# Twelve of an expert's fourteen weight loads move from the join to the next expert's first tile

## The chip, the cores and the metric

The kernel runs on one core of a Trainium2 chip. The metric is device microseconds of one execution, and the number that counts is the median of several runs. TensorE (PE) multiplies, VectorE (DVE) and ScalarE (ACT) do the element work, GpSimd (POOL) issues the indirect transfers, SyncE (SP) issues the plain ones.

## The reference

Causal attention (4 batches, 12 heads, 448 positions, 64 wide) gives 1792 rows of 768. Two mixture-of-experts layers follow, each with 8 experts whose weights are 768x1024 and 1024x768. In the first layer a row is computed only if its skip score is above 0; each row goes to the one expert with the largest logit:

```
for e in range(E):
    mask = e_idx == e
    h = np.maximum(xc[mask] @ w1[e], 0.0)
    y[mask] = gate_w[mask, None] * (h @ w2[e])
out[do_compute] = xc + y
```

The second layer does the same with all rows, normalised logits and other weights, and without adding the row itself.

## The kernel before

The attention is written out first and takes about the first 230 us. The rest is 16 experts, 8 of each layer, in one order written out by hand for every engine (`tc.manual_schedule`). An expert's rows are taken in tiles of 128 by an indirect gather. How many tiles an expert has is known only at run time: `Tile.begin` and `Tile.finish` of a first tile are always there, further tiles stand in a branch (`tc.If(nmore[e] > 0)`, line 1107, and the tests of `middle`, line 1088). Behind the branch the paths join again, and there stands one `tile.finish(at_end, True, ...)` for whichever tile was the last of the expert (line 1118).

A tile works in this order on TensorE. `begin`: `layer1` (line 781) makes two halves of 512 columns from six chunks of w1, first the terms with the high part of the weights, then those with the low part; the halves are copied (line 940), turned (line 798) and split by ReLU into high and low (lines 772, 773); then `layer2` (line 789) goes through chunks 0 to 5 of w2. `finish`: the next tile's rows are turned and split (lines 754, 760, 761) between `layer2` of chunks 6 and 7, and the result is scaled and written out by `put_y`. In the first layer the routing of the second (`route_...`) is woven into the same tiles: `route_turn` (line 834, copied by ACT at line 835), `route_logits` (line 840), and a write of the row to `x2` (line 856).

Weights come in as float32 (`raw`) and are split into a rounded high part by ACT (line 736) and the remainder by DVE (line 740). The remainder overwrites the raw chunk. There are 14 rooms for w1 chunks (`N1`, six chunks per expert) and 16 for w2 chunks (`N2`, eight per expert), so a load at expert i brings chunks 2 to 5 of w1 of expert i+2, chunks 0 and 1 of w1 of expert i+3, and all of w2 of expert i+2. A w1 chunk is 512 KB, a w2 chunk 384 KB. `load1` (line 212) and `load2` (line 218) issue on SP's queue, which in this stage carries nothing but these loads and SP's own branches. Each waits until the products that read the old content of its room are done.

In an expert's first tile the high parts of w2 are made at `w2_high(0, 1, 2, 3)` (in `begin`, before the first products), `w2_high(4)` and `w2_high(5, 6, 7)`; those of the next expert's w1 at `ahead(0)`, `ahead(1)` and, in `finish` of the last tile, `high(2)` to `high(5)`.

`paced(load, after)` can put a load behind a named instruction; in the kernel before no call passes one.

Between the layers stands a turn (lines 1137 to 1158): the last rows are routed, `dispatch` gathers the first tile of expert 8 (line 743, by `first`), and TensorE runs products of zeros (`busy`, line 129) in the meantime.

Of the kernel before, what the change touches and what calls it, by code (L numbers as in the profile page):

```python
# [26 lines left out]
KC = DM // P  # L27
FC = DF // P
# [17 lines left out]
def moe_attention_kernel(tc, qk, vv, w_r, emb, tau, w11, w12, w21, w22, out):  # L46
    nc = tc.nc
# [24 lines left out]
    with ExitStack() as top:  # L72
# [135 lines left out]
        def load1(n, after=None):  # L208

            if n < len(experts) * KC:  # L210
                (m, e), k = experts[n // KC], n % KC
                paced(nc.sync.dma_start(raw1[n % N1], wsrc[m][0][e, k * P : (k + 1) * P, :]), after)

        def load2(n, after=None):

            if n < len(experts) * FC:
                (m, e), f = experts[n // FC], n % FC
                paced(nc.sync.dma_start(raw2[n % N2], wsrc[m][1][e, f * P : (f + 1) * P, :]), after)
# [466 lines left out]
        with ExitStack() as ctx:  # L685
# [7 lines left out]
            for n in range(FC, N2):  # L693
# [20 lines left out]
            gate2 = keep([P, 1], F32, "gate2")  # L714
            norms = (keep([P, 1], F32, "ss2"), keep([P, 8], F32, "ex2"), keep([P, 1], F32, "gs2"),
                     keep([P, 1], I32, "tn_y"), keep([P, 1], F32, "tn_a"))
            state = {"tp": 0}

            def next_tp():
                state["tp"] = (state["tp"] + 1) % 3  # L720
# [54 lines left out]
            def layer1(i, u, ks, low):  # L775

                for k in ks:
                    wh, wl, _ = w1(i, k)
                    terms = [(0, wl)] if low else [(0, wh), (1, wh)]
                    for j, r in terms:  # L780
                        nc.tensor.matmul(p1[u], xt[:, k, :, j], r[:, u * 512 : (u + 1) * 512],  # L781
                                         start=(k == 0 and j == 0 and not low), stop=(k == KC - 1 and low))

            def layer2(i, f, us=(0, 1)):
                wh, wl, _ = w2(i, f)
# [156 lines left out]
            class Tile:  # L942
# [23 lines left out]
                def ahead(self, k):  # L966

                    if self.first and self.i + 1 < len(experts):
                        split_high(self.i + 1, k)
                        split_low(self.i + 1, k, nc.vector)  # L970

                def begin(self):
                    i, route = self.i, self.m == 0 and self.prev
                    if self.m == 1 and self.prev:
                        put_out()
                    self.step()
                    self.w2_high(0, 1, 2, 3)
                    layer1(i, 0, range(4), False)
                    layer1(i, 1, range(3), False)
                    layer1(i, 0, range(4, KC), False)  # L980
                    self.step()
                    layer1(i, 0, range(KC), True)
                    if route:

                        route_enter()
                    self.w2_low(0, 1)
                    copy_h(0)
                    self.w2_high(4)
                    self.step()
                    self.w2_low(2, 3)  # L990
                    self.step()
                    layer1(i, 1, range(3, KC), False)
                    if i == 0 and not self.prev:
                        late_hots()
                        enter_late()
                    if route:
                        route_turn()
                    state["tp"] = 2
                    turned = turn_h(0)
                    self.step()  # L1000
                    split_ht(turned, 0)
                    while self.norm:
                        self.step()
                    layer1(i, 1, range(KC), True)
                    copy_h(1)
                    self.w2_high(5, 6, 7)
                    if route:
                        route_logits()
                    self.w2_low(4)
                    if route:  # L1010
                        route_pick()
                    self.w2_low(5)
                    layer2(i, 0)
                    layer2(i, 1)
                    turned = turn_h(1)
                    split_ht(turned, 4)
                    self.w2_low(6, 7)
                    layer2(i, 2)
                    layer2(i, 3)
                    if route:  # L1020
                        route_rank()
                    self.ahead(0)
                    self.ahead(1)
                    layer2(i, 4)
                    layer2(i, 5)

                def finish(self, idx, last, nxt, route):
                    i = self.i
                    more = last and i + 1 < len(experts)
                    state["tp"] = 1  # L1030

                    def high(*ks):
                        for k in ks:
                            if more:
                                split_high(i + 1, k)

                    def low(*ks):
                        for k in ks:
                            if more:
                                split_low(i + 1, k, nc.vector)  # L1040

                    if last:
                        for k in range(KC):
                            load1(KC * i + k + N1)
                        for f in range(FC - 2):
                            load2(FC * i + f + N2)
                    if nxt is not None:
                        t = xt_turn(nxt, *HALVES[0])
                        xt_split(t, *HALVES[0])
                    high(2)  # L1050
                    layer2(i, 6)
                    if nxt is not None:
                        t = xt_turn(nxt, *HALVES[1])
                        xt_split(t, *HALVES[1])
                    low(2)
                    high(3)
                    low(3)
                    layer2(i, 7)
                    if last:
                        load2(FC * i + 6 + N2)  # L1060
                        load2(FC * i + 7 + N2)
                    high(4, 5)
                    low(4, 5)
                    if route:
                        route_put()
                    put_y(self.m, self.g, idx)

            def run_layer(m, info, ir):
                L, _, _, nmore, several = info
                for e in range(NE):  # L1070
                    i, c0 = m * NE + e, e * CT

                    prev = e > 0

                    def rows(t):
                        return L[:, c0 + t : c0 + t + 1]

                    gr, gr2 = g_r[e % 2], g_r[(e + 1) % 2] if e + 1 < NE else None
                    at_end = ir[:, e : e + 1]
                    tc.mark_branch_hint_location(f"more{i}", several[e], engines=list(nc.engines))  # L1080
                    if gr2 is not None:
                        gather(m, gr2, rows(CT))
                    gather(m, g_n[1], rows(1))
                    tile = Tile(i, gr, True, prev)
                    tile.begin()

                    def middle(t):
                        with tc.If(nmore[e] > t):  # L1088
                            g = g_n[t % 2]
                            if t <= NMID:  # L1090
                                g2 = g_n[(t + 1) % 2]
                                gather(m, g2, rows(t + 1))
                                mid = Tile(i, g, False, True)
                                mid.begin()
                                mid.finish(rows(t), False, g2, m == 0)
                                middle(t + 1)
                            else:
                                with tc.For_i(t, nmore[e], 1) as u:
                                    nc.vector.tensor_copy(ix, L[:, bass.ds(u + c0, 1)])
                                    gather(m, g, ix)  # L1100
                                    make_xt(g)
                                    mid = Tile(i, g, False, True)
                                    mid.begin()
                                    mid.finish(ix, False, None, m == 0)
                                make_xt(gr)

                    with tc.If(nmore[e] > 0, label=f"more{i}"):
                        if m == 1:
                            gather(m, gr, at_end)
                        tile.finish(rows(0), False, g_n[1], m == 0 and prev)  # L1110
                        if m == 0:
                            gather(m, gr, at_end)
                        middle(1)
                        end = Tile(i, gr, False, True)
                        end.begin()
                        if m == 0 and not prev:
                            route_put()
                    tile.finish(at_end, True, gr2, m == 0 and prev)

            with tc.manual_schedule():  # L1120
# [86 lines left out]
```

## Time and profile before

| what | us |
|---|---|
| median of 3 runs (901.76 to 904.38) | 903.12 |
| the profiled execution's own time | 902.78 |
| its span, first to last instruction | 901.1 |
| TensorE busy in it | 824.0 |
| VectorE busy | 554.4 |
| ScalarE busy | 474.8 |

The profiled execution is 0.34 us under the median and lies 1.7 us over its own span. The mean granted TensorE clock is 0.978 of full speed. TensorE is busy in nearly all of the span, so idle stretches of the other engines cost something only where TensorE ends up waiting for them.

### The profile page before, as it was taken

What the parts mean: (1) busy time and instruction counts of PE and PEld (TensorE: products, weight loads), DVE (VectorE), ACT (ScalarE), POOL (GpSimd) and SP (SyncE); (2) the same over time, 40 slices, a digit from 0 to 9 for tenths busy, and PEclk for the clock granted to TensorE, in tenths of its full rate; (3) what the DMA queues carried; (4) which work ended last, traced back from release to release, by engine and by line L of the source; (5) the groups of instructions that cost most, each with busy time, mean ns of one, the idle gap of its engine ahead of it and who ended that gap; (6) DMA issues with size and microseconds to landing.
All of it is one profiled execution on the core that took longest, in us unless ns stands there. A gap on an engine that the chain in (4) does not pass through costs nothing. (4 is left out here: it accounts for less than half of the span.)

```text
span 901.1 us, 14898 instructions
## 1 busy us (share of the span) xinstructions
PE 824.0 (91%) x4960; PEld 686.5 (76%) x4960; DVE 554.4 (62%) x1641; ACT 474.8 (53%) x1013; POOL 135.2 (15%) x150
## 2 busy tenths in 40 slices
PE   7998989989797899899999879899999998999994
PEld 5665766666487788788899748789889887889884
DVE  5767767776566688378833476665283268574343
ACT  5777666666455466166612336454272256463252
POOL 1132404013201111011010021011111011110100
PEclk9999999999899899999999999999999999999998
DMA  8979565563636487267710354580451086361000
GB/s 243 315 271 299 165 185 165 167 206 139 202 140 258 175 300 286 72 232 300 299 45 28 145 198 159 197 332 21 149 211 51 19 313 267 133 238 41 37 1 18
DMA packets 59032, 158.22 MB, mean 176 GB/s; under 512 B 13013, under 2 KB 23765, under 8 KB 58448
## 3 DMA queue, kind: packets, MB, share of 16 engines
q1 hardware_dynamic: 52816, 139.33, 43.4%
q0 software_dynamic: 6080, 17.29, 5.4%
q8 instruction: 59, 0.97, 0.5%
q14 instruction: 77, 0.63, 0.2%
HBM read 146.45 MB, written 22.92 MB: 188 GB/s over the span
## 5 line engine op out<-in xcount | busy, mean ns | idle before, releaser
L789 PE MATMUL p<-hi,ht 128*128 128x384 f32 x960 | 241.8, 353 | 8.5 <-DVE ht L773 4.6
L740 DVE TENSOR_TENSOR lo<-raw,hi 128x768 fp32r<-128x768 f32 (+1 forms) x218 | 220.6, 1062 | 8.0 <-ACT hi L736 4.5
L781 PE MATMUL p<-hi,xt 128*128 128x512 f32 x720 | 183.3, 403 | 8.0 <-PEq L1088 3.3
L736 ACT CAST hi<-raw 128x768 fp32r<-128x768 f32 (+1 forms) x218 | 187.3, 923 | 0.6 <-DMA raw<-in_w 0.6
L789 PEld LDWEIGHTS p<-hi,ht 128*128 128x128 f32 x960 | 167.8, 191 | 14.7 <-DVE ht L773 10.6
L781 PEld LDWEIGHTS p<-hi,xt 128*128 128x128 f32 x720 | 140.4, 198 | 37.4 <-ACTq L1088 5.1
L321 ACT ACTIVATE pr<-st,mn 112x336 f32<-112x336 f32 x192 | 99.5, 520 | 60.4 <-DVE mn L318 60.4
L789 PE MATMUL p<-lo,ht 128*128 128x384 f32 x480 | 124.3, 340 | 0.4 <-issue 0.4
L773 DVE SCALAR_TENSOR_TENSOR ht<-tp,ht 128x512 fp32r<-128x512 f32 x60 | 41.4, 689 | 115.3 <-ACT ht L772 106.6
L781 PE MATMUL p<-lo,xt 128*128 128x512 f32 x360 | 96.2, 402 | 0.0
L940 ACT COPY hs<-p 128x512 f32<-128x512 f32 x60 | 34.8, 580 | 106.0 <-PE p L781 67.0
L789 PEld LDWEIGHTS p<-lo,ht 128*128 128x128 f32 x480 | 88.7, 191 | 0.5 <-issue 0.5
L760 ACT CAST xt<-tp 128x384 fp32r<-128x384 f32 (+2 forms) x62 | 30.4, 492 | 109.5 <-PE tp L754 108.8
L761 DVE TENSOR_TENSOR xt<-tp,xt 128x384 fp32r<-128x384 f32 (+2 forms) x62 | 33.3, 544 | 84.5 <-ACT xt L760 81.6
L318 DVE CUSTOM_DVE_ANT_0 st<-s,mask 112x336 f32<-112x336 f32 x144 | 63.5, 465 | 29.4 <-PE s L307 17.8
L781 PEld LDWEIGHTS p<-lo,xt 128*128 128x128 f32 x360 | 67.8, 195 | 11.4
L772 ACT ACTIVATE ht<-tp 128x512 fp32r<-128x512 f32 x60 | 36.0, 600 | 55.1 <-PE tp L798 49.4
L331 PE MATMUL tp<-ident,pr 112*112 112x112 f32 x480 | 57.3, 267 | 0.0
L307 PE MATMUL s<-qk 64*112 64x112 f32 (+2 forms) x288 | 49.6, 450 | 7.1 <-DVE mn L318 7.1
L331 PEld LDWEIGHTS tp<-ident,pr 112*112 112x112 f32 x480 | 47.1, 136 | 8.6 <-issue 7.8
L818 POOL DMA_INDIRECT out<-py,pidx x18 | 19.7, 1093 | 207.7 <-ACT hi L736 75.5
L342 PE MATMUL av<-pt,v 112*64 112x448 f32 (+3 forms) x384 | 50.6, 405 | 0.0
(201 smaller groups left out, 908.3 us busy)
## 6 DMA issues: line engine op xcount, KB each, us to landing
raw<-in_w SPq DMA_DIRECT2D x96, 512.0 KB
raw<-in_w SPq DMA_DIRECT2D x128, 384.0 KB
qk<-in_qk SPq DMA_DIRECT2D x23, 896.0 KB
x<-x SPq DMA_DIRECT2D x24, 448.0 KB
v<-in_vv SPq DMA_DIRECT2D x4, 1344.0 KB
qk<-in_qk SPq DMA_DIRECT2D x2, 448.0 KB
g_n<-x,L POOLq DMA_INDIRECT x23, 4.4
out<-py,pidx POOLq DMA_INDIRECT x18, 3.4
```

The lines of the kernel that those rows point to most:

```text
L307: nc.tensor.matmul(a[c], src[r : r + 64, c * CP : (c + 1) * CP], src[r : r + 64, S : S + n], start=True, stop=True)
L318: nc.vector.tensor_tensor_reduce(out=so, in0=a[c], in1=mask[:, S - n : S], scale=-0.125, scalar=3.0e38, op0=ALU.add, op1=ALU.min, accum_ou ...
L321: return lambda: nc.scalar.activation(a["pr"][:, OFF[c] * CP : OFF[c] * CP + n], so, AF.Exp, bias=mn, scale=-1.0, accum_out=rs)
L331: nc.tensor.transpose(tp[:, u * CP : (u + 1) * CP], pr[:, o : o + CP], ident[:CP, :CP])
L342: nc.tensor.matmul(av[u * D : (u + 1) * D, j * CP :], v_t[b][:, j, 2 * hp + u, :], pts[2 * g + u][:, o : o + (NCH - j) * CP], start=(j == ...
L736: copy(hi, raw)
L740: eng.tensor_tensor(lo, raw, hi.bitcast(F32), op=ALU.subtract)
L772: nc.scalar.activation(hi, src, AF.Relu)
L773: nc.vector.scalar_tensor_tensor(lo, src, 0.0, hi.bitcast(F32), op0=ALU.max, op1=ALU.subtract)
L781: nc.tensor.matmul(p1[u], xt[:, k, :, j], r[:, u * 512 : (u + 1) * 512], start=(k == 0 and j == 0 and not low), stop=(k == KC - 1 and low))
L789: mm = nc.tensor.matmul(p2[u], l, r[:, u * (DM // 2) : (u + 1) * (DM // 2)], start=(f == 0 and j == 0), stop=(f == FC - 1 and j == len(ter ...
L940: nc.scalar.copy(hs[:, u * 512 : (u + 1) * 512], p1[u])
```

## The change

Of the fourteen loads that `finish` issued at the join, the first two w1 chunks stay. The other four w1 chunks and the eight w2 chunks are put in a list. The first tile of the next expert takes one of them behind each of twelve pieces of its products: four pieces of `layer1` with high parts and low parts of the first half and the start of the second, two more of the second half, and `layer2` of chunks 0 to 5. Each load then waits, by `paced`, for the last product of its piece. `layer1` now returns the name of its last product.

```diff
-            state = {"tp": 0}
+            state = {"tp": 0, "loads": []}
+
+            def feed(after):
+
+                if state["loads"]:
+                    load, n = state["loads"].pop(0)
+                    load(n, after)
...
-                        nc.tensor.matmul(p1[u], xt[:, k, :, j], r[:, u * 512 : (u + 1) * 512],
+                        mm = nc.tensor.matmul(p1[u], xt[:, k, :, j], r[:, u * 512 : (u + 1) * 512],
                                          start=(k == 0 and j == 0 and not low), stop=(k == KC - 1 and low))
+                return mm.ins.name
...
+                def feed(self, after):
+                    if self.first:
+                        feed(after)
...
-                    layer1(i, 0, range(4), False)
-                    layer1(i, 1, range(3), False)
-                    layer1(i, 0, range(4, KC), False)
+                    self.feed(layer1(i, 0, range(4), False))
+                    self.feed(layer1(i, 1, range(3), False))
+                    self.feed(layer1(i, 0, range(4, KC), False))
...
-                    layer1(i, 0, range(KC), True)
+                    self.feed(layer1(i, 0, range(KC), True))
...
-                    layer1(i, 1, range(3, KC), False)
+                    self.feed(layer1(i, 1, range(3, KC), False))
...
-                    layer1(i, 1, range(KC), True)
+                    self.feed(layer1(i, 1, range(KC), True))
...
-                    layer2(i, 0)
-                    layer2(i, 1)
+                    self.feed(layer2(i, 0))
+                    self.feed(layer2(i, 1))
...
-                    layer2(i, 2)
-                    layer2(i, 3)
+                    self.feed(layer2(i, 2))
+                    self.feed(layer2(i, 3))
...
-                    layer2(i, 4)
-                    layer2(i, 5)
+                    self.feed(layer2(i, 4))
+                    self.feed(layer2(i, 5))
...
                     if last:
-                        for k in range(KC):
-                            load1(KC * i + k + N1)
-                        for f in range(FC - 2):
-                            load2(FC * i + f + N2)
+                        load1(KC * i + N1)
+                        load1(KC * i + 1 + N1)
+                        state["loads"] = [(load1, KC * i + k + N1) for k in range(2, KC)]
+                        state["loads"] += [(load2, FC * i + f + N2) for f in range(FC)]
...
-                    if last:
-                        load2(FC * i + 6 + N2)
-                        load2(FC * i + 7 + N2)
```

The first tile of an expert comes before its branch in every engine's order, so the twelve loads are issued whether the expert has one tile or more. The first tile of expert 0 finds the list empty.

## Rows read from the trace of the kernel before

**Rows 1.** The page: busy time of the engines.

```profile
PE 824.0 (91%) x4960; PEld 686.5 (76%) x4960; DVE 554.4 (62%) x1641; ACT 474.8 (53%) x1013; POOL 135.2 (15%) x150
```

**Rows 2.** Stretches, one tile each: length; busy by engine; clock; DMA share; GB/s.

```profile
core 0: us, PE busy (x) PEld busy (x) DVE busy (x) ACT busy (x) POOL busy (x), PEclk, DMA share, GB/s
263.83:291.43 27.60, 22.48 (x120) 19.91 (x120) 19.68 (x33) 16.37 (x24) 3.45 (x3) 0.95 0.74 277
291.43:319.63 28.20, 24.29 (x121) 21.96 (x121) 19.14 (x39) 14.76 (x22) 3.46 (x3) 0.87 0.49 191
388.83:411.18 22.35, 20.94 (x121) 18.71 (x120) 19.77 (x40) 15.60 (x23) 3.45 (x3) 1.00 0.48 183
411.18:433.53 22.35, 20.94 (x121) 18.73 (x121) 19.78 (x40) 15.62 (x23) 4.49 (x4) 1.00 0.79 304
```

**Rows 3.** Timeline of PE, experts 1, 2 and 6: start, length, what, idle before.

```profile
279.43 0.65 PE L798 MATMUL tp<-ident,hs 128*128 128x128 f32 x4 [2.38 <-ACT hs L940]
287.26 0.52 PE L754 MATMUL tp<-ident,g_r 128*128 128x128 f32 x3 [2.74 <-DVEq L1107]
305.16 1.20 PE L840 MATMUL pm<-wr,yt 128*128 128x8 f32 x6 [3.22 <-ACT yt L835]
...
408.40 0.52 PE L754 MATMUL tp<-ident,g_r 128*128 128x128 f32 x3 [1.24 <-DVEq L1107]
```

**Rows 4.** Timeline of ACT, experts 1, 2 and 6.

```profile
278.79 0.58 ACT L940 COPY hs<-p 128x512 f32<-128x512 f32 x1 [5.91 <-issue]
304.63 0.48 ACT L835 COPY yt<-tp 128x384 f32<-128x384 f32 x1 [4.86 <-issue]
...
421.35 0.58 ACT L940 COPY hs<-p 128x512 f32<-128x512 f32 x1 [0.82 <-PE p L781]
```

**Rows 5.** Timeline of SP at the join of expert 0.

```profile
260.69 2.78 SPq L212 DMA_DIRECT2D raw<-in_w  x6
263.58 8.94 SPq L218 DMA_DIRECT2D raw<-in_w  x8
```

**Rows 6.** Short stretches (columns as in rows 2; the last three: clock, DMA share, GB/s).

```profile
276.00:278.00 2.00, 1.05 (x6) 0.73 (x5) 0.37 (x2) 0.00 (x0) 0.66 (x1) 1.00 1.02 378
278.00:280.00 2.00, 0.57 (x5) 0.58 (x6) 0.00 (x0) 1.21 (x2) 0.00 (x0) 1.00 0.20 72
302.00:304.00 2.00, 0.00 (x0) 0.00 (x0) 0.00 (x0) 0.00 (x0) 0.00 (x0) 1.00 0.25 87
318.00:334.00 16.00, 15.82 (x91) 14.08 (x90) 14.90 (x34) 12.86 (x19) 3.46 (x3) 1.00 1.01 384
```

**Rows 7.** The page: a DMA queue that brings instructions (packets, MB, share).

```profile
q14 instruction: 77, 0.63, 0.2%
```

**Rows 8.** The turn: timelines of POOL, DVE and PE.

```profile
524.00 0.99 POOL L856 DMA_INDIRECT x<-py,pidx  x1 [12.23 <-DVE eq L848]
530.12 1.45 POOL L743 DMA_INDIRECT g_r<-x,first  x1 [5.13 <-DMA x<-py,pidx]
...
527.37 0.22 DVE L197 TENSOR_SCALAR first<-pm,tok 128x1 int32<-128x1 f32 x1 [0.30 <-PE pm L878]
...
534.61 1.54 PE L754 MATMUL tp<-ident,g_r 128*128 128x128 f32 x6 [2.77 <-DMA g_r<-x,first]
```

**Rows 9.** Line 856, all its writes to x2: landing times.

```profile
DMA to landing us min/median/max: 2.5/3.1/3.3
```

**Rows 10.** Stretches around the turn (columns as in rows 2).

```profile
517.00:526.00 9.00, 6.77 (x43) 4.92 (x42) 6.59 (x26) 4.87 (x9) 0.99 (x1) 1.00 1.02 407
530.00:537.60 7.60, 4.83 (x20) 3.44 (x18) 5.70 (x9) 2.00 (x5) 4.13 (x3) 0.78 0.37 107
```

**Rows 11.** Timelines of PE and ACT in expert 7's first tile.

```profile
433.53 4.35 PE L781 MATMUL p<-hi,xt 128*128 128x512 f32 x18
451.33 0.51 PE L789 MATMUL p<-hi,ht 128*128 128x384 f32 x2
...
444.18 2.30 ACT L736 CAST hi<-raw 128x768 fp32r<-128x768 f32 x3
```

**Rows 12.** Branches: PE timeline at expert 4's second tile; a stretch over a join.

```profile
365.58 1.86 PE L781 MATMUL p<-hi,xt 128*128 128x512 f32 x6 [0.96 <-DVEq L1088]
...
594.00:598.00 4.00, 4.00 (x23) 3.70 (x22) 2.63 (x4) 3.98 (x6) 0.00 (x0) 1.00 1.02 417
```

More of the change, by code (lines that the diff above doesn't have):

```diff
@@ L1117, in run_layer @@
                             route_put()
+                    assert not state["loads"]
                     tile.finish(at_end, True, gr2, m == 0 and prev)
```

## The prediction

> **What bounds the kernel now.** I read the page first: TensorE is busy 824.0 of 901.1 us [rows 1], so a change that adds and removes no product can only win or lose in TensorE's idle stretches and in its clock. The second view is a table of stretches, each from the first product of one tile to that of the next [rows 2]. The reader should compare the lengths. Single-tile experts of the first layer take 22.35 us with the DMA engines 48% busy and 22.35 us with them 79% busy: transfers as such slow nothing. But the tiles of experts 1 and 2 take 27.60 and 28.20 us for the same 120 or so products. They are 5.25 and 5.85 us too long, 11.10 us together.
>
> The third view, TensorE's timeline, shows where [rows 3]. In expert 1's tile it waits 2.38 us for ACT's copy of the second half (line 940) and 2.74 us at the join, where 1.24 us is usual. In expert 2's it waits 3.22 us for ACT's copy at line 835. The first two give 2.38 + (2.74 - 1.24) = 3.88 us; the rest is the clock, granted at 0.95 and 0.87 of full speed in these stretches and 1.00 in the others [rows 2]: 0.05 x 27.60 = 1.4 us, together 5.3 us, as found. For expert 2, 3.22 us and 0.13 x 28.20 = 3.7 us make 6.9 us, less what the shorter join gives back.
>
> Now ACT's own timeline [rows 4]. It is idle for 5.91 us before the one copy and 4.86 us before the other, and both times the releaser is "issue": it waited for no semaphore that the profile shows. In expert 6 the same copy starts after 0.82 us, as soon as TensorE is done. So something withholds ACT's next instruction. The short stretches say what ends it [rows 6]: up to 278 us the DMA engines are full (share 1.02), in the next 2 us they fall to 0.20, and ACT goes on at 278.79; in 302 to 304 us they are at 0.25, and ACT goes on at 304.63. Instructions come over DMA queues too [rows 7], and what fills the engines is the burst: SP issues fourteen loads within 11.8 us of the join [rows 5], 6 x 512 KB + 8 x 384 KB = 6.29 MB, which at 384 GB/s [rows 6] take 16.4 us. My reading: a block of ACT's instructions, asked for near the join, stands behind that burst, and ACT stops when it comes to the block's edge before the block is there. In the other experts the edge falls elsewhere or the block was fetched ahead of the burst.
>
> **The change part by part.**
>
> *The burst is cut to two loads.* 1.05 MB at 384 GB/s take 2.7 us, so a block asked for at the join is there some 3 to 4 us later, well ahead of the copies, which come 10 us and more behind the join. Later, four loads of 512 KB come behind pieces that end about 1.9 to 6 us after the first product (the first eighteen products of the first three pieces take 4.35 us [rows 11]): 2.10 MB, 5.5 us of transfer, so a queue of about 2 us at most. The last eight come about one per 1.2 us, each worth 1.02 us. Nothing stands long enough to hold back ACT by 5 us. I take both tiles down to the usual 22.35 us: -11.1 us. Bounds: 0 (the cause is another one) and -11.1.
>
> *The turn between the layers.* Expert 7's burst keeps the DMA engines at 1.02 in 517 to 526 us [rows 10]. The write to `x2` issued at 524.00 holds up the gather of expert 8's first rows until 530.12 [rows 8], 6.1 us, where such writes land after 2.5 to 3.3 us [rows 9]. TensorE then waits 2.77 us for that gather [rows 8], and the clock is at 0.78 over 7.6 us around it [rows 10], 1.7 us. With only two loads there, the write lands by 524.00 + 3.3 = 527.3 and the next thing late is `first`, ready at 527.37 + 0.22 = 527.59 [rows 8]. The gather could move up by 530.12 - 527.6 = 2.5 us; most of that and part of the clock come back. I take -3 us, with bounds 0 and -4.4 (2.77 and 1.7).
>
> *The loads come later: does a split wait?* The last load goes out when the twelfth piece ends, at 451.33 + 0.51 = 451.84 in expert 7's first tile. Its user is the last of the three casts that start at 444.18, at about 445.7 [rows 11], one whole tile later: 445.7 + 22.35 = 468.1 us for a single-tile expert, the tightest case. That leaves 16.2 us for a transfer of 1.02 us. The first w1 chunk of the list is due a whole tile after its piece. All fourteen need 16.4 of 22.35 us of DMA time. Cost 0; were the cover gone, a late chunk would show as ACT waiting for `raw`.
>
> *Twelve waits on SP.* What is queued behind a waiting load is the next load and SP's branches; no other engine waits for SP but through the loads' landing, just priced. Issue is about 0.46 us a load (2.78 us for six [rows 5]), off the path. POOL's gathers and writes keep their order, and share the DMA engines with loads in the second half of the tile that were there in the first half before. TensorE gets no instruction that I can see: its products already signal to others. 0.
>
> *The end of the first tile.* This is new: loads now run until shortly before each first tile's branch, where the engines jump and need the code behind the jump. At such a branch with empty DMA engines TensorE waits 0.96 us for another engine's jump, and at the join of expert 9, with the DMA engines full (1.02), it is busy all 4.00 of 4.00 us [rows 12]. So a full DMA need not hurt there. Low end 0; high end: the last two loads (0.79 MB, 2.0 us) stand in front of the code at each of the 14 first tiles that issue loads (experts 1 to 14) and nothing covers it, +28 us. The row with full engines is the nearest, and the products of two more w2 chunks still follow the last load; I take +1.5 us in all.
>
> *Sum.* 902.78 (the profiled execution, 0.34 us under the median) - 11.1 - 3 + 1.5 = 890.2; against the median 890.5 us.
>
> What speaks against this is a rule of the Trainium skill, page "Runtime: NRT & Kernel Launch", section "Instruction fetch mechanics": the sequencer fetches its next block over a DMA queue of its own while it runs the present one, and the cost of crossing a block's edge is "mostly hidden". By that rule the two ACT stops would not be code at all, and the sum would lose its first term. The trace speaks against it: it has two idle stretches of about 5 us with no semaphore behind them, which the rule does not explain. The same page's remark that a taken branch breaks the fetching ahead fits a block asked for only at the join; no row here shows when it was asked for.
>
> **The rivals.**
>
> *Only part comes back.* ACT's block is asked for later than I think, or meets the four 512 KB loads (5.5 us of transfer): one of the two stops stays, 5.3 to 5.9 us, or the turn gives nothing. For it: the rows show when ACT went on, not when it asked. 902.8 - 5.5 - 1.5 + 1.5 = 897 us. Chance 0.17.
>
> *The stops have another cause.* ACT would stop in experts 1 and 2 whatever DMA does, or the waits for TensorE come out so that the loads still leave together. Against it: twice the engines drained just before ACT went on. The turn's gain and the branch's cost stay: 902.8 - 3 + 1.5 = 901.3 us. Chance 0.11. This is where that page's rule leads, too.
>
> *Slower: the code at the branch.* Each first tile's last loads hold up the code behind its branch. It decides from about 1 us per first tile beyond what the last two w2 chunks' products cover: 14 x 1.0 us cancels the gain of 14.1, and at the full 2.0 us the time is 902.8 - 14.1 + 28 = 917 us. Against it: the full engines at expert 9's join. Chance 0.08.
>
> **How the numbers follow.** The forecast has 0.64: 890.5 us, and its own range is 886.5 to 896 (both gains whole, or the branch costs up to 5 us more). The range 886.5 to 899.5 takes in the partial case, 0.81 together. A measurement of this kernel can tell about 0.3%, 2.7 us: 900.4 to 905.8 is no change. Faster: forecast, partial case and a little of the third, 0.82. Same: 0.10. Slower: 0.08.
>
> **What would show it.** Right: the tiles of experts 1 and 2 at 22.3 to 23 us with the clock at 1.00; no ACT idle of over 2 us ended by "issue" there; SP's twelve loads spread over some 18 us of each first tile; the gather of expert 8's first rows at about 528 us on the old scale; TensorE's waits at lines 1088 and 1107 no longer than now. Wrong: the same two ACT stops beside half-empty DMA engines, ACT or DVE waiting for `raw`, or TensorE waits of 2 us at every first tile's end.

## The result, and the profile after

The changed kernel takes 907.72 us (median of 20 runs) against 903.15 us for the kernel before (20 runs): the ratio is 1.0051, 95% interval 1.0031 to 1.0071. It is slower by about half a per cent, where 890.5 us and a gain were forecast. The profiled execution took 907.67 us with a span of 906.0 us, 4.9 us over the span of before.

The page shows first that the work is the same and only its timing has moved:

```profile
PE 827.5 (91%) x4960; PEld 688.5 (76%) x4960; DVE 554.6 (61%) x1641; ACT 474.6 (52%) x1013; POOL 137.7 (15%) x150
...
q1 hardware_dynamic: 52816, 139.33, 46.4%
```

The second line is SP's loads: packets, MB and the share of the DMA engines' time. The bytes are those of before. TensorE is busy for 3.5 us more with the same 4960 products [rows 1], so most of the 4.9 us are products at the lower clock (mean 0.972, before 0.978) and about 1.4 us are idle time. The next view is the table of stretches, one tile each, with the columns of [rows 2]: experts 1 and 2, expert 6, then the first and second tiles of experts 4, 9 and 13.

```profile
262.75:288.77 26.02, 22.34 (x120) 20.13 (x120) 19.18 (x33) 15.91 (x23) 6.63 (x3) 0.93 0.77 257
288.77:316.95 28.18, 23.97 (x121) 21.69 (x121) 19.62 (x39) 15.23 (x23) 3.46 (x3) 0.88 0.63 203
...
408.81:431.75 22.94, 20.95 (x120) 18.74 (x120) 19.77 (x40) 15.59 (x23) 4.48 (x4) 1.00 0.90 302
...
339.28:363.04 23.76, 20.93 (x121) 18.67 (x120) 22.18 (x53) 14.42 (x21) 3.65 (x4) 1.00 0.79 268
363.04:386.46 23.42, 22.45 (x120) 19.90 (x120) 3.76 (x12) 5.42 (x10) 1.87 (x2) 0.93 0.19 64
...
553.99:577.15 23.16, 19.26 (x101) 16.50 (x99) 20.08 (x42) 16.58 (x27) 2.86 (x3) 1.00 0.90 334
577.15:597.15 20.00, 20.00 (x99) 18.00 (x100) 4.37 (x18) 4.88 (x10) 2.41 (x3) 0.91 0.34 114
...
756.54:779.50 22.96, 19.05 (x100) 16.42 (x98) 19.84 (x41) 16.22 (x27) 3.06 (x3) 1.00 0.79 279
779.50:799.45 19.95, 19.95 (x99) 17.93 (x100) 4.21 (x17) 4.85 (x10) 2.23 (x3) 0.91 0.30 100
```

The same pairs of tiles in the kernel before, from the same view:

```profile
341.99:364.13 22.14, 20.93 (x120) 18.67 (x120) 20.82 (x48) 14.41 (x21) 3.46 (x3) 1.00 0.63 244
364.13:388.83 24.70, 22.76 (x120) 19.89 (x121) 5.09 (x18) 5.42 (x10) 2.05 (x2) 0.93 0.44 153
555.65:577.09 21.44, 19.19 (x99) 16.44 (x99) 19.54 (x38) 15.60 (x25) 2.21 (x2) 1.00 0.82 318
577.09:596.20 19.11, 18.63 (x98) 16.87 (x99) 4.81 (x22) 5.77 (x12) 3.06 (x3) 1.00 0.55 210
755.17:775.79 20.62, 19.34 (x99) 16.78 (x99) 18.71 (x37) 14.89 (x24) 2.26 (x2) 0.98 0.72 281
775.79:794.27 18.48, 18.48 (x98) 16.88 (x99) 4.83 (x22) 5.78 (x12) 3.04 (x3) 1.00 0.56 207
```

Read them as differences. Expert 1's tile has gained 27.60 - 26.02 = 1.6 us and expert 2's nothing (28.20 and 28.18), where 5.3 and 5.9 us were forecast. Expert 6's has lost 0.6 us. The pairs have lost: expert 4 from 46.84 to 47.18 us (+0.3), expert 9 from 40.55 to 43.16 us (+2.6), expert 13 from 39.10 to 42.91 us (+3.8). Together that is +5.7 us, against +4.9 us of the whole span. Each of these lengths is of one profiled execution. The clock column shows part of the loss: the second tiles of experts 9 and 13 had 1.00 before and have 0.91 now.

TensorE's timeline says what stands at these places: the join of expert 1, the copy of expert 2, the join of expert 6, and the second tiles of experts 4, 9 and 13.

```profile
284.42 0.54 PE L760 MATMUL tp<-ident,g_r 128*128 128x128 f32 x3 [3.68 <-DVEq L1115]
302.23 1.45 PE L847 MATMUL pm<-wr,yt 128*128 128x8 f32 x6 [3.08 <-ACT yt L842]
428.96 0.52 PE L760 MATMUL tp<-ident,g_r 128*128 128x128 f32 x3 [1.81 <-DVEq L1115]
...
363.04 6.00 PE L787 MATMUL p<-hi,xt 128*128 128x512 f32 x18 [2.67 <-PEq L1096]
577.11 5.28 PE L787 MATMUL p<-hi,xt 128*128 128x512 f32 x15 [2.52 <-PEq L1096]
779.46 4.83 PE L787 MATMUL p<-hi,xt 128*128 128x512 f32 x13 [2.66 <-PEq L1096]
```

Lines 1096 and 1115 are the branches of before's lines 1088 and 1107. "PEq" is TensorE's own sequencer: TensorE waits for its own jump. In the kernel before, the waits at the same branch were 1.06, 0.87 and 0.89 us (experts 4, 9 and 13; the first two are shown):

```profile
364.13 0.48 PE L781 MATMUL p<-hi,xt 128*128 128x512 f32 x1 [1.06 <-PEq L1088]
...
577.09 2.62 PE L781 MATMUL p<-hi,xt 128*128 128x512 f32 x10 [0.87 <-PEq L1088]
```

At expert 4 a second wait of 0.96 us, for DVE's jump, stood behind the first [rows 12]; the changed kernel has none there, which is why expert 4 lost so little. The views of the two lines show the jump itself (nanoseconds, shortest, median and longest), before and after:

```profile
L1088 PEldq COMPARE_BRANCH  x18: 65/188/3787, 360.2 to 851.8; - x18
...
L1096 PEldq COMPARE_BRANCH  x18: 65/186/5397, 357.5 to 857.0; - x18
```

A jump that takes 186 ns as a rule took 5.4 us at expert 4, from 357.5 us on, where the same jump took 3.8 us before. The DMA engines were then still busy with the first tile's last loads (share 0.96 in 355 to 361 us).

The trace also keeps each DMA packet with its queue and start, and these show what the jump waits for. In each of the three long jumps one packet of 16 KB comes on the instruction queue q8. In the kernel before, with the DMA engines nearly idle, it starts 1.0 us after the jump does, at all three places. In the changed kernel, with the engines full, it starts 2.2, 2.4 and 2.8 us after it. So the longer jump is a block of code that stands behind loads.

ACT's two stops are still there, shorter in expert 1 than the 5.91 us of before, nearly the same in expert 2 [rows 4]:

```profile
274.84 0.59 ACT L947 COPY hs<-p 128x512 f32<-128x512 f32 x1 [3.04 <-issue]
...
301.69 0.48 ACT L842 COPY yt<-tp 128x384 f32<-128x384 f32 x1 [4.73 <-issue]
```

At both places, before and after, an 8 KB packet on the other instruction queue, q14 [rows 7], starts 1.4 to 1.7 us before ACT goes on. So both stops end with a block of code.

The short stretches show what the spread did to the DMA engines there (last three columns: clock, DMA share, GB/s):

```profile
263.60:265.40 1.80, 1.80 (x10) 1.49 (x9) 1.80 (x3) 1.80 (x3) 0.00 (x0) 1.00 0.06 16
266.00:275.00 9.00, 9.00 (x54) 7.90 (x53) 8.82 (x20) 5.03 (x9) 5.60 (x2) 1.00 0.92 313
292.00:300.00 8.00, 7.15 (x40) 5.95 (x38) 7.23 (x20) 3.67 (x6) 2.43 (x2) 1.00 0.96 308
```

In the middle of the tiles, where ACT comes to its stops, the DMA engines are as full as before (0.92 and 0.96), though they move only 308 to 313 GB/s. Before it was 384 to 407 GB/s [rows 6, 10]. And in 263.6 to 265.4 us they were idle (0.06), 7 us before ACT stopped: a block asked for at the join would have come then.

At the turn the transfers did as forecast and the time did not. The gather of expert 8's first rows, from POOL's timeline, and TensorE's products of zeros:

```profile
527.59 1.05 POOL L749 DMA_INDIRECT g_r<-x,first  x1 [2.88 <-DVE first L197]
```

```profile
528.16 6.24 PE L129 MATMUL p<-zeros 128*68 128x476 bf16 x16 [1.11 <-issue]
534.24 0.82 PE L760 MATMUL tp<-ident,g_r 128*128 128x128 f32 x6
```

The same products in the kernel before, and the clock over them in the changed kernel:

```profile
528.44 3.40 PE L129 MATMUL p<-zeros 128*68 128x476 bf16 x16 [1.11 <-issue]
...
527.00:534.00 7.00, 5.89 (x16) 2.75 (x16) 5.21 (x8) 0.81 (x2) 3.47 (x3) 0.51 0.40 116
```

The gather no longer waits for the write but for `first`, 2.5 us earlier than in [rows 8]. But the sixteen products of zeros that fill the wait took 6.24 us instead of 3.4 us: the clock was granted at 0.51 in 527 to 534 us, its lower level of 1.2 GHz. TensorE came to the gathered rows at 534.24 us, 0.37 us earlier than before, and the 2.5 us were gone. Expert 7's last tile had lost time as well: it began 1.8 us earlier than before, at 494.43 us, and had a clock of 0.88 up to 508.5 us where it had 1.00 before, so that `first` was ready only 0.3 us earlier. From its start to that of expert 8's first tile it is 39.58 us before and 40.45 us after.

### The profile page after: what moved, and what is told of

It reads as the page before. It is cut to its first block, busy times and chain, and to the rows that moved or that the text cites. A ratio compares the mean times of both kernels' runs of the same rounds, so it can differ in the third digit from the quotient of the medians.

```text
span 906.0 us, 14886 instructions
## 1 busy us (share of the span) xinstructions
PE 827.5 (91%) x4960; PEld 688.5 (76%) x4960; DVE 554.6 (61%) x1641; ACT 474.6 (52%) x1013; POOL 137.7 (15%) x150
## 3 DMA queue, kind: packets, MB, share of 16 engines
q1 hardware_dynamic: 52816, 139.33, 46.4%
## 5 line engine op out<-in xcount | busy, mean ns | idle before, releaser
L787 PE MATMUL p<-hi,xt 128*128 128x512 f32 x720 | 186.1, 408 | 11.6 <-PEq L1096 8.3
L787 PEld LDWEIGHTS p<-hi,xt 128*128 128x128 f32 x720 | 142.3, 201 | 41.6 <-ACT yt L914 5.8
```

What stands on the lines that cost most here:

```text
L787: mm = nc.tensor.matmul(p1[u], xt[:, k, :, j], r[:, u * 512 : (u + 1) * 512], start=(k == 0 and j == 0 and not low), stop=(k == KC - 1 and ...
```

## The experiments

All ratios are to the kernel before, run on the same chip.

**Loads early in the tile (e1_early).** The twelve loads go two by two behind the first six pieces, so that none starts in `layer2`.

```diff
-                if state["loads"]:
-                    load, n = state["loads"].pop(0)
-                    load(n, after)
+                for _ in range(2):
+                    if state["loads"]:
+                        load, n = state["loads"].pop(0)
+                        load(n, after)
```

> The changed kernel, with the twelve loads two by two behind the first six pieces (all of layer1) instead of one by one behind twelve. Theory A (code blocks come over the same DMA engines and stand behind weight loads; the loads that run to the end of a first tile hold up the code behind its branch): TensorE's waits at line 1096 in experts 4, 9 and 13 (2.67, 2.52, 2.66 us with the change) fall back to about 1 us and the clock holds there; ACT's stops in experts 1 and 2 (3.0 and 4.7 us) stay, since the engines are as full as before in the middle of the tile: about 902 to 904 us. Theory B (the twelve waits on SP or the signals from TensorE cost the time, not the traffic): as with the change, about 907.5 us.

Measured: 904.18 us against 902.85, ratio 1.0018 (0.9996 to 1.0041). TensorE's waits at the same branch (line 1097 here) in experts 4, 9 and 13, from its timeline:

```profile
366.75 0.48 PE L788 MATMUL p<-hi,xt 128*128 128x512 f32 x1 [0.72 <-PEq L1097]
...
578.59 2.60 PE L788 MATMUL p<-hi,xt 128*128 128x512 f32 x10 [0.90 <-PEq L1097]
...
777.53 2.74 PE L788 MATMUL p<-hi,xt 128*128 128x512 f32 x10 [0.78 <-PEq L1097]
```

They are back at 0.7 to 0.9 us, with the same twelve waits on SP; the packet of q8 starts 1.0 us after the jump, as before the change. ACT's stops are 5.72 and 4.79 us, and the tiles of experts 1 and 2 take 27.0 and 27.2 us.

```profile
283.19 0.58 ACT L948 COPY hs<-p 128x512 f32<-128x512 f32 x1 [5.72 <-issue]
```

Theory A holds at the branch, and B does not. At ACT's first stop A expected 3.0 us; two loads at a time made it nearly the 5.91 us of the burst.

**Loads late in the tile (e2_late).** As before, but the first six pieces take no load and the last six take two each.

```diff
+                state["piece"] += 1
+                for _ in range(2 if state["piece"] > 6 else 0):
```

> The changed kernel, with the twelve loads two by two behind the last six pieces (layer2 of chunks 0 to 5). Theory A: no load is in flight when ACT comes to its block edges in experts 1 and 2, so both stops go and the tiles take about 22.4 us (-9.5 us); but more loads are in flight at the branches, where TensorE's waits in experts 4, 9 and 13 grow to 3 to 6 us and more first tiles may stop: between 898 and 910 us. Theory B: ACT's stops stay at 3 to 5 us, as in both kernels so far.

Measured: 915.49 us against 902.85, ratio 1.0147 (1.0120 to 1.0173), above the 898 to 910 us that were expected. The branch waits grew as theory A says, and the packet of q8 now starts 3.5 to 3.9 us after the jump; the branch is line 1100 here:

```profile
360.50 5.03 PE L789 MATMUL p<-hi,xt 128*128 128x512 f32 x11 [3.24 <-PEq L1100]
...
579.16 4.61 PE L789 MATMUL p<-hi,xt 128*128 128x512 f32 x10 [3.39 <-PEq L1100]
...
783.40 2.90 PE L789 MATMUL p<-hi,xt 128*128 128x512 f32 x6 [3.78 <-PEq L1100]
```

The joins behind single-tile first tiles grew too, to 4.86 us for expert 1 and 4.26 us for expert 6, which was not in the expectation. The tiles of experts 1 and 2 took 28.0 and 23.1 us, not about 22.4. ACT's stop in expert 2 no longer shows as one ended by "issue", and TensorE's wait there fell from 3.08 to 0.75 us. But ACT still stopped for 2.97 us in expert 1 with no load in flight (DMA share 0.02 in 271.6 to 273.3 us):

```profile
274.62 0.59 ACT L949 COPY hs<-p 128x512 f32<-128x512 f32 x1 [2.97 <-issue]
```

So theory A was right about the traffic and too simple about the edge: it costs something with idle DMA engines as well.

**The burst without its loads (e3_no01).** The kernel before, without the fourteen loads at the joins of experts 0 and 1; the missing chunks are split from a constant. Part of the weights of experts 2 to 4 is left out, so the total time says nothing and only the tiles of experts 1 and 2 are read.

```diff
-                            load1(KC * i + k + N1)
+                            if i < 2:
+                                gone1.add(KC * i + k + N1)
+                            else:
+                                load1(KC * i + k + N1)
```

> The kernel before without the fourteen loads at the joins of experts 0 and 1; the chunks that are missing are split from a constant (part of the weights of experts 2 to 4 of the first layer is left out, so later routing differs; only the tiles up to expert 3 of the first layer are compared). Theory A: without a burst ACT's stops in experts 1 and 2 shrink to what an edge costs with idle DMA engines, at most 3 us, and the tiles take 22.3 to 23.2 us instead of 27.6 and 28.2. Theory C: 27 to 28 us again.

Measured, from the stretches and ACT's timeline:

```profile
267.80:292.50 24.70, 22.34 (x120) 20.13 (x120) 19.35 (x33) 16.07 (x23) 6.63 (x3) 0.93 0.02 3
292.50:315.00 22.50, 20.94 (x121) 18.73 (x120) 19.33 (x39) 15.07 (x23) 3.47 (x3) 1.00 0.16 55
```

```profile
279.89 0.59 ACT L954 COPY hs<-p 128x512 f32<-128x512 f32 x1 [3.03 <-issue]
```

Expert 2's tile falls from 28.20 to 22.50 us: nearly all its excess over 22.35 us came from the burst. Expert 1's falls to 24.70 us and not to 23.2 us or less. With DMA engines at 0.02 of their time ACT still stops for 3.03 us. That is what this edge costs by itself; the burst adds 5.91 - 3.03 = 2.9 us.

**ACT's code moved by 32 instructions (e4_shift32, e6_shift).** The kernel before with 32 tiny copies on ACT, first all ahead of the attention, then where ACT is idle: 10 ahead of it, 22 behind the split of expert 0's first rows.

```diff
+            shift = const.tile([P, 1], F32, name="shift")
+            nc.vector.memset(shift, 0.0)
...
+                for _ in range(10):
+                    nc.scalar.copy(shift, shift)
                 busy_here(12)
...
                 make_xt(g_r[0])
+                for _ in range(22):
+                    nc.scalar.copy(shift, shift)
```

> The kernel before, with 32 tiny ACT copies ahead of the attention, so that every later ACT instruction stands 32 places further on in ACT's code. Theory A with block edges: the stops leave the copies at lines 940 and 835 of experts 1 and 2 and move to an instruction 32 places earlier, or into code that is jumped over; if the latter, both tiles take 22.4 us and the time is about 892 us plus up to 2 us for the 32 copies. Theory C (the stops belong to these instructions or to their operands): 27.6 and 28.2 us again, about 903 us.

> The kernel before with the 32 tiny ACT copies placed where ACT is idle: 10 before the first attention head, while it waits for its input, and 22 behind the split of expert 0's first rows, where it waits 5.3 us for TensorE. Theory A with block edges: the tiles of experts 1 and 2 take 22.2 to 22.6 us as in the run with all 32 ahead, and the 7 us that the copies cost there are gone: about 892 us. Theory C (the gain there had another source): 900 to 903 us.

Measured: 896.30 us against 902.85, ratio 0.9924 (0.9901 to 0.9946), with all copies ahead; they take 7.1 us there, before the first head, and not the 2 us that were expected. Where ACT is idle: 893.87 us against 902.37, ratio 0.9909 (0.9875 to 0.9943). Stretches of the second:

```profile
263.10:285.30 22.20, 20.89 (x121) 18.73 (x121) 18.84 (x32) 15.65 (x23) 6.62 (x3) 1.00 0.79 299
285.30:307.70 22.40, 20.98 (x121) 18.75 (x119) 19.82 (x40) 15.59 (x23) 3.46 (x3) 1.00 0.76 292
```

Not one product, load or wait of the two tiles was changed, the DMA engines are as full as before (0.79 and 0.76), and both tiles are down to the usual length, with the clock at 1.00. ACT's copy of the second half (line 940 before) starts 0.82 us after ACT is free, as in expert 6. So the stops belonged to places in ACT's code, and theory C falls. In this profile the two tiles are 11.2 us shorter than before and the whole span only 8.4 us: expert 7's last tile with the turn, and expert 8's tile, took 3.4 us more.

The label "issue" alone does not prove an edge. In all the kernels ACT also stops for 4.1 to 4.2 us at the turn, ended by "issue", with no packet of q14 in it, and moving the code left that stop as it was.

**The changed kernel with the same 32 copies (e7_after_shift), and the early loads with them (e8_early_shift).**

> The changed kernel with the same 32 copies. Theory A: the tiles of experts 1 and 2 fall to about 22.4 us, the waits at line 1096 in experts 4, 9 and 13 stay at 2.5 us and more with the clock falling behind them: about 898 us, 5 to 7 us over the kernel before with these copies. Theory D (the spread costs nothing but through ACT's edges): as the kernel before with these copies, 892 us.

> The changed kernel with the loads two by two behind the first six pieces, and the same 32 copies. Theory A: no ACT stops and short branch waits: 891 to 893 us, as the kernel before with these copies. Theory B (the paced waits cost time by themselves): above 895 us.

Measured: the changed kernel with the copies takes 900.34 us, ratio 0.9986 (0.9963 to 1.0010); the early loads with the copies take 894.25 us, ratio 0.9895 (0.9865 to 0.9926). Both kernels have the same loads and the same number of waits. In the first, TensorE's timeline still shows

```profile
357.07 0.48 PE L791 MATMUL p<-hi,xt 128*128 128x512 f32 x1 [1.83 <-PEq L1100]
...
570.16 2.04 PE L791 MATMUL p<-hi,xt 128*128 128x512 f32 x4 [2.63 <-PEq L1100]
...
770.72 1.77 PE L791 MATMUL p<-hi,xt 128*128 128x512 f32 x4 [2.48 <-PEq L1100]
```

With ACT's edges out of the way, the spread is worth 900.34 - 893.87 = +6.5 us against the burst: that is its own price, as theory A expected (5 to 7 us), and theory D falls. The profiles of the two runs show where it lies. Experts 4, 9 and 13 took 1.6, 2.2 and 3.1 us more than in e6_shift. Expert 1's tile took 24.8 us, where A expected 22.4 and e6_shift has 22.2: its join waited 2.52 us for DVE's jump (1.31 in e6_shift), and the clock fell behind that. The turn and what follows it gave part back. In the second kernel the branch waits are 0.91, 1.07 and 0.77 us. Its time lies between A's 891 to 893 us and B's "above 895", 0.4 us above e6_shift, the burst with the same copies, and well within the noise. These two, e6_shift and e8_early_shift, are faster than both kernels of this case; their intervals do not tell them apart.

**The waits without the traffic (e5_small).** The changed kernel, each paced load cut to 32 KB into a scrap tile; the missing chunks are split from a constant. This part of the weights is left out, and the rows then go to other experts: the second layer has one tile more, so its total time (914.94 us) cannot be compared, only the first layer's tiles.

```diff
+                if after is not None:
+                    gone1.add(n)
+                    paced(nc.sync.dma_start(scrap, wsrc[m][0][e, k * P : (k + 1) * P, 0:64]), after)
+                    return
```

> The changed kernel with all its waits, but each of the twelve paced loads brings 32 KB into a scrap tile instead of 512 or 384 KB, and the splits of the chunks that are then missing read a constant (this part of the weights is left out). Theory A: with a thirteenth of the traffic ACT's stops in experts 1 and 2 go (-9.5 us) and TensorE's waits at line 1096 fall to about 1 us (-5 us): about 891 to 894 us. Theory B: 907 us, nothing changes but the traffic.

```profile
262.90:286.00 23.10, 20.77 (x121) 18.63 (x120) 18.84 (x32) 15.49 (x23) 6.63 (x3) 1.00 0.11 29
286.00:308.80 22.80, 21.06 (x120) 18.76 (x120) 19.84 (x40) 15.58 (x23) 3.45 (x3) 1.00 0.24 72
```

Experts 1 and 2 take 23.1 and 22.8 us instead of 26.0 and 28.2, and the branch wait in expert 4 is 0.96 us (2.67 with full loads):

```profile
353.35 0.47 PE L810 MATMUL p<-hi,xt 128*128 128x512 f32 x1 [0.96 <-PEq L1119]
```

A wait of 1.07 us for DVE's jump follows it, as in the kernel before. All twelve waits on SP are still there. ACT still stops for 3.08 us in expert 1. The cost is the traffic's; B falls a second time.

## Why the prediction was wrong

*What bounds the kernel:* right. TensorE's idle stretches and its clock hold everything that moved, and ACT's two stops are blocks of its code that come over the DMA engines (the packets of q14, e3_no01, e6_shift). The 11.1 us were there to be had: the two tiles are 11.2 us shorter in e6_shift, and the medians of e6_shift and e8_early_shift lie 8.5 and 8.1 us under the kernel before. The working for expert 2 does not close: 3.22 + 3.7 us, less 0.55 us for the shorter join, make 6.4 us and not 5.85.

*"The burst is cut to two loads": wrong, -11.1 us forecast, -1.6 us found in the two tiles.* The step that failed is "a block of ACT's instructions, asked for near the join", and with it the price of 0 for an edge without a burst. The block did not come near the join: the DMA engines were idle in 263.6 to 265.4 us of the changed kernel and ACT still stopped at 272; with no traffic at all the edge still costs 3.03 us. The packets agree. In e2_late, e3_no01 and e5_small, with the engines nearly idle, the packet of q14 starts 1.6 us after ACT stopped in expert 1, and in the changed kernel it does so too; in the kernel before it starts 4.4 us after. When it was asked for, no trace shows; at the join the engines were free to bring it.

In expert 1 the burst's share of the stop is therefore gone (5.91 to 3.04 us) although the engines were full; the bare edge stayed, and the join behind it rose from 2.74 to 3.68 us. In expert 2 what the traffic adds stayed whole (4.73 after 4.86 us): the packet starts 3.2 us after the stop in both kernels, as the transfers of the spread run on through ACT's edge, some 8 to 9 us into the tile, like those of the burst. There "a queue of about 2 us at most" was too small: with idle engines ACT waits 1.9 to 2.4 us at this place, so the loads add 2.3 us and more. It took 384 GB/s for granted, and the spread loads moved 308 to 313.

*The turn: right in the transfers, wrong in the sum.* The write no longer held the gather, which moved to 527.59 us as worked out (527.6). That the two agree so closely is partly luck: the tile began 1.8 us earlier and lost 1.5 us of that to the clock. The step that failed is "most of that and part of the clock come back": the row of products of zeros in front of the gathered rows ran at half clock. The clock fell there after a stretch with several short waits that both kernels have. In the profiles of e7_after_shift and e8_early_shift, also with early transfers, expert 7's last tile and the turn took 37.9 and 38.4 us against 41.6 us in e6_shift, so the gain can be had in some executions. What decides when the clock falls stays open.

*A split that waits for its weights:* right at 0. No wait for `raw` is left in the expert stage of the changed kernel.

*Twelve waits on SP:* right at 0 within the noise (e8_early_shift has them all and takes as long as e6_shift; e5_small has them too).

*The end of the first tile: mis-sized, +1.5 us forecast, +6.5 us found (e7_after_shift against e6_shift).* Rival three had the mechanism, a chance of 0.08 and a price of 28 us over 14 tiles. What the runs show is the same mechanism at fewer places: in the changed kernel's profile three first tiles (experts 4, 9, 13: +0.3, +2.6, +3.8 us, clock included) and some joins (+0.6 us in expert 6). The row that I took as nearest, the full DMA engines at expert 9's join with TensorE busy throughout [rows 12], was the wrong neighbour: TensorE's jump there took 0.18 us, and no instruction packet moved between 585 and 604 us, so nothing was fetched that a load could hold up. The nearest row was the other one, the branch with idle engines. Its 0.96 us was the wait for DVE's jump; the wait of 1.06 us for TensorE's own jump, 1.5 us before it, was missed, and it is what grew at experts 4, 9 and 13. The series settles it: with the last loads early the branch waits 0.7 to 0.9 us, spread 2.5 to 2.7, late 3.2 to 3.8.

The page "Runtime: NRT & Kernel Launch" of the Trainium skill, section "Instruction fetch mechanics", says that a taken branch out of the code at hand forces a fetch before execution goes on. The trace agrees: the jump of 5.4 us has a 16 KB packet of q8 inside it. The same section of the Trainium skill calls the cost of crossing a block's edge "mostly hidden". That does not hold at two of ACT's edges here: at the first it stopped 3.03 us with idle DMA engines and 5.91 us with full ones. But q14 carried 77 packets in all [rows 7], and but for the stop at the turn no other stop of ACT in the expert stage that "issue" ended is over 1.2 us, before or after. The rival by which the stops have another cause falls with the packets of q14 and with e6_shift.

## What to carry to other kernels

Code came over the same DMA engines as weights here, so a transfer that nobody waits for can still stop an engine: keep the DMA engines idle where the program jumps, and where an engine that others wait for crosses a block of its code. Spreading a burst evenly is the wrong shape for that; a burst that ends well before the branch was better than an even stream, by 4.6 us here and by 6.5 us with ACT's code moved. Where one engine stops with no semaphore behind it, moving its code by a few instructions (32 here) is a cheap test, and here it was also the best change. The place is this program's own: any later change to ACT's code moves its edges again. The source gives the branch of line 1107 a hint (`tc.mark_branch_hint_location`) and that of line 1088 none; whether a hint there would shorten the jump, no run shows.

## What the runs showed of the hardware that was not expected

One block's edge cost ACT about 3 us with idle DMA engines (3.03, 3.08 and 2.97 us in three kernels), so this block was not there ahead of time.

With the DMA engines nearly idle, TensorE's jump waited 1.0 us for the start of its 16 KB packet; behind loads, in the changed kernel and e2_late, it waited 2.2 to 3.9 us.

Loads issued one at a time filled the DMA engines' time (share 0.92 to 0.96) at 308 to 313 GB/s; the same loads in a burst moved 384 to 407 GB/s. SP's loads took 46.4% of the engines' time instead of 43.4% for the same 139.33 MB.

Half clock ran sixteen products of zeros in 6.24 us instead of 3.40, right where they were put in to bridge a wait: a filler of fixed count became the bound itself.
